# Regrouping the weight transform of a frequency-domain convolution: groups of four frequencies, three matmuls of 160 columns per PSUM bank

## The chip, the cores and the metric

The kernel runs on one core of a Trainium2 chip. The metric is the device time of one execution in microseconds (us). The time before is the median of three runs, 275.3 us, with a lowest of 274.16 us and a highest of 279.05 us. The profile is of one further execution, which took 277.49 us and whose span from the first to the last instruction was 275.8 us.

## The reference

```
H = W = 224; C = 96; K = 7            # x: (1, 224, 224, 96) bf16, w: (7, 7, 96, 96) bf16
wp = pad w with zeros to (224, 224, 96, 96)
Xf = rfft2(x over H and W); Wf = rfft2(wp over H and W)
Yf = einsum('bhwi,hwio->bhwo', Xf, Wf)
y  = irfft2(Yf) as bf16                # (1, 224, 224, 96)
```

This is a circular 7 x 7 convolution of an image of 96 channels into 96 channels. Every output channel sums over every input channel, tap by tap.

## The kernel before, in words

**What is computed where.** The rows are cut into 8 blocks (NJ) of 28 output rows. Each block is transformed along H by a short transform of length 34, which gives NS = 17 frequencies; frequency 0 carries two real parts, every other one three parts (real, imaginary, and a difference of the two, so that a complex product takes three real ones). Along W the kernel stays in the position domain and works with taps: the 7 taps and three sums of neighbouring taps, NTAP = 10, used on even positions, odd positions and their differences. The width is cut into 7 tiles of 32 pixels. For each tile t and frequency s, `b_round(t, s)` does the products over the 96 input channels: 33 matmuls of 96 columns (22 for frequency 0) with the pixels as the stationary operand and the transformed weights `WF` as the moving one. ScalarE scales the first bank (`tt_`), VectorE makes `u` and `v`, GpSimd (for some rounds VectorE) adds them into `yf`, and after each group of frequencies `yf` goes to a scratch tensor in DRAM, from which `tt` is read back in another layout for the inverse transform (`Gm`) and the output.

**Forward transform of the pixels.** Matmuls with `Fm` on pixel rows (`xn`) put the frequencies of a tile into PSUM, and an eviction writes them to `xf`. VectorE then makes the planes of differences and sums, `J`, for a group of three frequencies at a time (`jit`).

**Transform of the weights, where the change is.** `WF` holds, for each of 50 slots (frequency and part) and 10 taps, a 96 x 96 matrix. It is made once, group by group of frequencies (`PGRP`, line 31). `prep_jobs(gi)` (lines 322 to 359) makes one job per PSUM bank. A job takes hb pairs of output channels; for each pair one matmul has the raw weights `wq` as stationary operand, 98 rows by 128 columns, whose columns stand 96 elements (192 bytes) apart (`wqx[0:PW2, o:o + 127 * C + 1:C]`, line 340), and as moving operand the small table `Em`, which selects taps and multiplies by cosines and sines. Each matmul gives both channels of the pair, 10 taps, and two parts of each frequency of the group. One eviction per bank, from fp32 in PSUM to bf16, then writes hb neighbouring output channels for each slot and tap:

```
evac(wv[:, :, 0:2 * NTAP, :, o0:o1],
     pv_.rearrange("i k h (s q) -> i s q h k", s=ns), NB * ncol)
```

so the innermost run of the write is hb elements of bf16, starting at element o0 = ob * hb of a row of 48. The third part of each frequency is a subtraction on VectorE over 960 elements (`diff(s)`, line 353). In all groups before, NB = 8 and hb = 4: twelve banks to a group, four matmuls to a bank. A group of three frequencies has matmuls of 2 x 3 x 2 x 10 = 120 columns and evictions of 480 elements; group 0 (frequencies 0 and 1, all five slots) has matmuls of 100 columns.

**What sets the order.** Everything is recorded in program order; there is no other scheduler. Tiles 0 and 1 run together, tile 1 four rounds behind (LAG = 4): round r does frequency r of tile 0, and from r = 4 also frequency r - 4 of tile 1. A clock k counts two steps per round (k = 2r, 2r + 1). Every batch of jobs is entered with `add(a, b, jobs)` and `pace` hands it out evenly over steps a to b - 1, in the middle and at the end of a round (`mid`, `end`). Group gi of the weights is due in the rounds of the group before it:

```
add(2 * PGRP[gi - 1][0], 2 * PGRP[gi - 1][1] - 1, pj)
...
k = 2 * (PGRP[gi][0] + i) - 2          # the subtraction of a frequency: one round ahead of its use
```

Before, group 2 is made in rounds 2 to 4, groups 3, 4 and 5 in rounds 5 to 7, 8 to 10 and 11 to 13. `f_jobs` and the copies of a halo bring tile 1's pixels in during rounds 1 to 6, and tile 2's from round 9.

**Which engine evicts.** `evac` (line 122) keeps a running cost of VectorE and ScalarE (`load`) and gives each eviction to the one that is behind; `load["p"]`, the cost of TensorE's work, lifts both when they lag behind it. So an eviction may change engine when the costs before it change.

**When the raw weights' memory is given up.** At r = PGRP[-2][1] + 1 the pool that holds `wq` is closed and the tiles for the inverse transform take its place; two GpSimd memsets (`GA`, `GB`) follow.

Of the kernel before, what the change touches and what calls it, by code (L numbers as in the profile page):

```python
# [25 lines left out]
NB = 8  # L26
# [1 line left out]
NTAP = 10  # L28
TAPS = ((7, 8, 9, 6), (0, 2, 4, 6), (1, 3, 5))
NSLOT = 2 + 3 * (NS - 1)  # L30
PGRP = ((0, 2), (2, 5), (5, 8), (8, 11), (11, 14), (14, 17))
YGRP = ((0, 3), (3, 6), (6, 9), (9, 12), (12, 15), (15, 17))
YGRPL = ((0, 3), (3, 6), (6, 9), (9, 12), (12, 15), (15, 17))
SA = 9
# [13 lines left out]
def slot(s, part):  # L48
    return part if s == 0 else 2 + 3 * (s - 1) + part
# [3 lines left out]
def kernel(  # L53
# [54 lines left out]
    def bank():  # L108
        return pools["psb"].tile([128, 512], F32, name="pb")
# [5 lines left out]
    def apart(key, zone, r):  # L115
        for z, q in parts.setdefault(key, []):
            if z != zone and q.engine != r.ins.engine:
                tc.declare_no_dep(r.ins, q, reason="disjoint parts of one tile")
        parts[key].append((zone, r.ins))
        return r  # L120

    def evac(out_ap, in_ap, n):
        if tail[0]:
            return tail_evac(out_ap, in_ap, n)
        cv, ca = 180 + 1.0 * n, 160 + 0.85 * n
        for k in "va":
            load[k] = max(load[k], load["p"])
        if load["v"] + cv <= load["a"] + ca:
            load["v"] += cv
            return VE.tensor_copy(out=out_ap, in_=in_ap)  # L130
        load["a"] += ca
        return SE.copy(out=out_ap, in_=in_ap)
# [34 lines left out]
    xh_bufs = [late[:, 2 * (XW + 32) + i * XHW:2 * (XW + 32) + (i + 1) * XHW] for i in range(2)]  # L167
    assert 2 * (XW + 32 + XHW) <= 8 * NTAP * C and NSLOT - 8 > slot(PGRP[-1][0], 0)

# [109 lines left out]
    VE.tensor_tensor(out=pv[:, :, 2], in0=pv[:, :, 0], in1=pv[:, :, 1], op=ALU.subtract)  # L279
    for k0, k1 in ((0, slot(PGRP[0][1], 0)), (slot(PGRP[0][1], 0), NSLOT)):  # L280
        VE.tensor_tensor(out=Em[:, :, k0:k1], in0=pe3[:, k0:k1].unsqueeze(1).unsqueeze(3).to_broadcast([PW2, 2, k1 - k0, NTAP]),
# [40 lines left out]
    def prep_jobs(gi):  # L322
        s0, s1 = PGRP[gi]
        ns = s1 - s0
        full = gi == 0
        ncol = (NSLOT_OF(s0, s1) if full else 2 * ns) * NTAP
        nb = C // NB
        hb = NB // 2
        assert NB * ncol <= 512 and C2 % hb == 0

        def mk_(ob):
            def f():
                pw = bank()
                pv_ = pw[:, 0:NB * ncol].rearrange("p (k h q) -> p k h q", h=2, q=ncol)
                ev = Em[:, :, slot(s0, 0):slot(s1 - 1, 2) + 1, :]
                ev = ev.rearrange("p h a t -> p h (a t)") if full else ev.rearrange("p h (s r) t -> p h s (r t)", r=3)[:, :, :, 0:2 * NTAP]
                load["p"] += 63.0 * hb
                for k in range(hb):
                    o = ob * hb + k
                    TE.matmul(pv_[:, k], lhsT=wqx[0:PW2, o:o + 127 * C + 1:C], rhs=ev, start=True, stop=True)  # L340
                pv_ = pv_[0:C]
                o0, o1 = ob * hb, (ob + 1) * hb
                wv = WF[0:C, slot(s0, 0):slot(s1 - 1, 2) + 1]
                if full:
                    wv = wv.rearrange("i a t (h o) -> i (a t) h o", h=2)
                    apart(("W", gi), ob, evac(wv[..., o0:o1], pv_.rearrange("i k h q -> i q h k"), NB * ncol))
                    return
                wv = wv.rearrange("i (s r) t (h o) -> i s (r t) h o", r=3, h=2)
                apart(("W", gi), ob, evac(wv[:, :, 0:2 * NTAP, :, o0:o1],
                      pv_.rearrange("i k h (s q) -> i s q h k", s=ns), NB * ncol))  # L350
            return f

        def diff(s):
            def f():
                load["v"] += 250 + C * NTAP / 1.92
                w0, w1, w2 = (WF[0:C, slot(s, r)].rearrange("i t o -> i (t o)") for r in range(3))
                VE.tensor_tensor(out=w2, in0=w0, in1=w1, op=ALU.subtract)
            return f
        return [mk_(ob) for ob in range(nb)], [] if full else [diff(s) for s in range(s0, s1)]

    def NSLOT_OF(s0, s1):
        return slot(s1 - 1, 2) + 1 - slot(s0, 0)
# [3 lines left out]
    def new_xf(t, s0=0, s1=NS):  # L366
        xf = xf_bufs[t % 2]
        xf_tiles[t] = xf
        if t > 0:
            prev = xf_tiles[t - 1]  # L370
            for ph in range(2):
                o, i = (v[0:C, ph, :, s0:s1, p:p + HALO, :].rearrange("c r s w j -> c r s (w j)") for v, p in ((xf, 0), (prev, TW)))
                apart(("A", t), ("halo", s0), SE.copy(out=o, in_=i))
                load["a"] += 160 + 0.85 * 2 * (s1 - s0) * HALO * NJ
        return xf
# [35 lines left out]
    def then_load(f, t, jg):  # L411
        def g():
            f()
            if t < NT:
                load_x(t, jg)
        return g
# [262 lines left out]
    def queue_c(t):  # L679
        pend.extend((t, *k) for k in LT)  # L680
        pump()
# [11 lines left out]
    for f in prep_jobs(0)[0]:  # L693
        f()
# [22 lines left out]
    def fills(qs, k):  # L717
        def f():
            for q in qs:
                pace(q, k)  # L720
        return f

    qs = []

    def add(a, b, jobs):
        qs.append([a, b, jobs, len(jobs)])

    for gi in range(1, len(PGRP)):
        pj, dj = prep_jobs(gi)
        add(2 * PGRP[gi - 1][0], 2 * PGRP[gi - 1][1] - 1, pj)  # L730
        for i, f in enumerate(dj):
            k = 2 * (PGRP[gi][0] + i) - 2
            add(k, k + 1, [f])
# [11 lines left out]
    for r in range(NS + LAG):  # L745
        if r == 0:
            add(0, 4, fj[1][1])
        for p in range(2):
            if r == (1, 3)[p]:
                new_xf(1, SH2[1][p], SH2[1][p + 1])  # L750
                fj = f_jobs(1, p)
                if p == 1:
                    for jg in range(2):
                        fj[jg][-1] = then_load(fj[jg][-1], 2, jg)
                add(2 * r + 1, 2 * r + (5, 8)[p], fj[0] + fj[1])
        for p in range(3):
            if r == (9, 14, 17)[p]:
                new_xf(2, SH2[2][p], SH2[2][p + 1])
                fj = f_jobs(2, p)
                if p == 2:  # L760
                    for jg in range(2):
                        fj[jg][-1] = then_load(fj[jg][-1], 3, jg)
                add(2 * r, 2 * r + (8, 7, 5)[p], fj[0] + fj[1])
        if r == PGRP[-2][1] + 1:
            assert not any(q[2] for q in qs[:4 * len(PGRP) - 8])
            wtmp_cm.__exit__(None, None, None)
            t_pool = ctx.enter_context(tc.tile_pool(name="tt", bufs=NTT, side="right"))
            t2_pool = ctx.enter_context(tc.tile_pool(name="tt2", bufs=1, side="right"))
            yo_pool = ctx.enter_context(tc.tile_pool(name="yo", bufs=2, side="right"))
            g_pool = ctx.enter_context(tc.tile_pool(name="gp", bufs=1, side="right"))  # L770
            GA = g_pool.tile([KA, 4 * B], BF16, name="GA")
            GB = g_pool.tile([128, 2, 4 * B], BF16, name="GB")
            GE.memset(GA[:], 0.0)
            GE.memset(GB[:], 0.0)
        if r == NS + 3:
            queue_c(0)
        for t in range(2):
            s = r - LAG * t
            if not 0 <= s < NS:
                continue  # L780
            now = bursts.pop((r, t), ())
            now = jit(*now) if now else ()
            both = LAG <= r < NS
            b_round(t, s, fills(qs, 2 * r + (t if both else 0)), fills(qs, 2 * r + (t if both else 1)), False, now)
# [8 lines left out]
    for t in range(2, NT):  # L793
# [6 lines left out]
        qs = []  # L800
# [100 lines left out]
```

## Time and profile before

| engine | busy, us | share of the span | instructions |
|---|---|---|---|
| TensorE, matmuls | 260.8 | 95% | 5088 |
| TensorE, weight loads | 238.9 | 87% | 5088 |
| VectorE | 227.8 | 83% | 469 |
| ScalarE | 196.3 | 71% | 475 |
| GpSimd | 102.2 | 37% | 152 |

The busy time of an engine is the union of its instructions' times, and matmuls overlap each other: one is listed at some 200 ns, while the next starts 42 ns later. So the distance from one start to the next, not the listed duration, tells what a matmul costs in a stream. The shares are means over stages with different limits. The chip's profile has 288 matmuls on `wq` (48 of 100 columns, 240 of 120 columns), between 18.4 and 80.2 us of the span. The rounds of tiles 0 and 1 fill the span from about 24 to 103 us; tiles 2 to 6 follow, 17 rounds each.

### The profile page before, as it was taken

How to read it: one execution, taken by the hardware profiler on the slowest of the kernel's cores; microseconds unless marked ns; L12 is line 12 of the kernel's file. 1: busy time of each engine (PE TensorE's matmuls, PEld its weight loads, DVE VectorE, ACT ScalarE, POOL GpSimd, SP SyncE). 2: the span in 40 equal slices, each digit the busy share in tenths (PEclk: the TensorE clock that was granted, in tenths of full speed). 3: DMA queues.
4: the chain of work that ended last, by engine and by line, in shares of the span. 5: the costliest groups of instructions: out<-in, count | busy, mean ns of one | idle time of the engine just before them, and what ended most of it. 6: DMA issues, size and time to landing. Idle time of an engine off the chain costs nothing.

```text
span 275.8 us, 12056 instructions
## 1 busy us (share of the span) xinstructions
PE 260.8 (95%) x5088; PEld 238.9 (87%) x5088; DVE 227.8 (83%) x469; ACT 196.3 (71%) x475; POOL 102.2 (37%) x152
## 2 busy tenths in 40 slices
PE   8969999989998999999999999999999999999972
PEld 3649998989998999899999999999999999999751
DVE  5528999998999889977976897788988889899933
ACT  5518997768774566898988869888887874653522
POOL 7720033445446455233243215222432242654200
PEclk9988999999999999999999999999999999999999
DMA  6954313411111189787979487977949833979775
GB/s 176 239 99 128 88 48 108 146 50 48 45 60 67 55 243 191 198 244 230 315 211 256 131 239 222 220 200 200 295 132 180 275 124 110 206 213 241 185 185 181
DMA packets 46211, 46.79 MB, mean 170 GB/s; under 512 B 35274, under 2 KB 37846, under 8 KB 46058
## 3 DMA queue, kind: packets, MB, share of 16 engines
q1 hardware_dynamic: 45692, 44.34, 59.3%
q0 software_dynamic: 464, 1.67, 1.8%
q8 instruction: 40, 0.66, 1.1%
q14 instruction: 15, 0.12, 0.1%
HBM read 24.65 MB, written 21.33 MB: 167 GB/s over the span
## 4 chain that ended last, share of the span: by engine, by line
PE 56%; DVE 17%; DMA 12%; issue 6%; ACT 4%; POOL 3%; SPq 2%; DVEq 0%
PE pb L87 56%; DVE J L87 6%; DMA wq<-in_w_dram 5%; DMA tt<-scr 5%; DVE WF L87 4%; DVE v L87 3%; POOL yf L87 3%; DVE u L87 2%; SPq L87 2%; ACT xf L87 2%; DMA xf<-scrl 2%; ACT WF L87 1%; DVE yf L87 1%; DVE yo L87 0%; DVE xf L87 0%
## 5 line engine op out<-in xcount | busy, mean ns | idle before, releaser
L87 PE MATMUL pb<-WF,J 96*128 96x96 bf16 x2898 | 167.6, 206 | 1.4 <-DVE J L87 0.6
L87 PEld LDWEIGHTS <-J 96*128 96x128 bf16 x2898 | 141.5, 98 | 10.7 <-DVE J L87 1.7
L87 POOL TENSOR_TENSOR yf<-v,u 128x384 bf16<-128x384 f32 x85 | 85.2, 1018 | 141.7 <-issue 84.8
L87 ACT CAST xf<-pb 96x408 bf16<-96x408 f32 (+5 forms) x142 | 66.9, 492 | 7.8 <-PE pb L87 5.8
L87 PE MATMUL pb<-WF,xf 96*128 96x96 bf16 x952 | 61.0, 206 | 2.9 <-DVE WF L87 2.1
L87 DVE TENSOR_TENSOR J<-xf 96x1824 bf16<-96x1824 bf16 (+1 forms) x84 | 60.3, 756 | 0.1
L87 PEld LDWEIGHTS <-xf 96*128 96x128 bf16 x952 | 47.4, 98 | 3.8 <-issue 3.1
L87 PE MATMUL pb<-Fm,xn 118*128 118x136 bf16 (+4 forms) x576 | 44.5, 203 | 0.0
L87 ACT CAST WF<-pb 96x480 bf16<-96x480 f32 (+1 forms) x60 | 30.0, 561 | 8.4 <-PE pb L87 8.1
L87 PE MATMUL pb<-tt,Gm 102*84 102x384 bf16 (+1 forms) x132 | 33.6, 327 | 0.0
L87 PEld LDWEIGHTS <-xn 118*128 118x128 bf16 x576 | 29.2, 98 | 0.1
L87 ACT CAST yo<-pb 84x384 bf16<-84x384 f32 (+1 forms) x61 | 26.3, 480 | 4.1 <-PE pb L87 4.0
L87 ACT CAST J<-pb 84x384 bf16<-84x384 f32 (+1 forms) x62 | 26.8, 482 | 2.7 <-PE pb L87 2.7
L87 DVE TENSOR_TENSOR J<-J 96x912 bf16<-96x912 bf16 (+1 forms) x42 | 24.9, 594 | 0.0
L87 PE MATMUL pb<-wq 98*128 98x120 bf16 (+1 forms) x288 | 22.9, 234 | 2.1 <-DMA wq<-in_w_dram 2.1
L87 PEld LDWEIGHTS <-wq 98*128 98x128 bf16 x288 | 20.5, 151 | 2.5 <-issue 2.5
L87 PE MATMUL pb<-wu 128*128 128x512 bf16 (+3 forms) x70 | 18.7, 398 | 1.1 <-DVE ct L87 1.1
L87 DVE TENSOR_TENSOR yf<-v,u 128x384 bf16<-128x384 f32 x27 | 15.6, 578 | 0.9
L87 DVE TENSOR_TENSOR WF<-WF 96x960 bf16<-96x960 bf16 x15 | 15.8, 1057 | 0.2
L87 PEld LDWEIGHTS <-wu 128*128 128x128 bf16 (+3 forms) x70 | 7.9, 115 | 8.4 <-issue 2.9
L87 DVE CAST WF<-pb 96x400 bf16<-96x400 f32 (+1 forms) x12 | 7.2, 608 | 8.4 <-PE pb L87 8.1
L87 PEld LDWEIGHTS <-Gm 102*84 102x84 bf16 (+1 forms) x132 | 11.5, 117 | 1.7 <-issue 0.6
(394 smaller groups left out, 236.9 us busy)
## 6 DMA issues: line engine op xcount, KB each, us to landing
scr<-yf SPq DMA_DIRECT2D x30, 288.0 KB
xn<-in_x_dram SPq DMA_DIRECT2D x12, 672.0 KB
tt<-scr SPq DMA_DIRECT2D x24, 336.0 KB
out_dram<-yo SPq DMA_DIRECT2D x12, 252.0 KB
out_dram<-J SPq DMA_DIRECT2D x12, 252.0 KB
tt<-scr SPq DMA_DIRECT2D x6, 288.0 KB
wq<-in_w_dram SPq DMA_DIRECT2D x1, 1719.0 KB
scrl<-yf POOLq DMA_DIRECT2D x5, 288.0 KB, 5.1
```

Source lines behind the costliest of these rows:

```text
L87: r = fn(*a, **k)
```

## The change

From group 2 on, a weight group has four frequencies instead of three. A matmul then has 2 x 4 x 2 x 10 = 160 columns, and since a PSUM bank holds 512 fp32 values, three of them fit instead of four: NB is 6 instead of 8 for these groups, hb is 3 instead of 4, and there are 16 banks to a group. The eviction of a bank still has 480 elements. There are five groups instead of six. The purpose is to make the same transformed weights with fewer matmuls and weight loads. An assertion is put in terms of the due step instead of an index.

```diff
-PGRP = ((0, 2), (2, 5), (5, 8), (8, 11), (11, 14), (14, 17))
+PGRP = ((0, 2), (2, 5), (5, 9), (9, 13), (13, 17))
@@ prep_jobs
         ncol = (NSLOT_OF(s0, s1) if full else 2 * ns) * NTAP
+        NB = 8 if ns < 4 else 6
         nb = C // NB
         hb = NB // 2
@@ rounds of tiles 0 and 1
         if r == PGRP[-2][1] + 1:
-            assert not any(q[2] for q in qs[:4 * len(PGRP) - 8])
+            assert not any(q[2] for q in qs if q[1] <= 2 * r)
```

## The prediction

> **What bounds the kernel now.** I read the page's slices first, to see which engine is full where the weights are made (18 to 80 us, slices 3 to 12).
>
> ```profile
> PE   8969999989998999999999999999999999999972
> DVE  5528999998999889977976897788988889899933
> ACT  5518997768774566898988869888887874653522
> ```
>
> Each digit is a fortieth of the span, 6.9 us. From slice 14 on TensorE is full and VectorE is not: TensorE sets the pace of tiles 2 to 6, which the change does not touch. From 28 to 62 us VectorE is as full as TensorE. So I asked for the busy time in stretches that end with the `v` of one round or two of tiles 0 and 1:
>
> ```profile
> 32.54:36.30 3.76, 3.76 (x91) 3.76 (x90) 3.76 (x8) 3.76 (x9) 1.57 (x1) 1.00 0.01 2
> 36.30:39.87 3.57, 3.57 (x83) 3.50 (x82) 3.15 (x7) 3.57 (x10) 1.00 (x1) 1.00 0.23 87
> 39.87:44.26 4.39, 3.85 (x87) 3.60 (x86) 4.29 (x9) 3.09 (x10) 1.39 (x2) 1.00 0.34 85
> 44.26:49.16 4.90, 4.90 (x112) 4.90 (x111) 4.90 (x9) 4.21 (x11) 1.66 (x2) 1.00 0.25 80
> 49.16:54.26 5.10, 5.10 (x119) 5.10 (x118) 5.02 (x10) 4.37 (x11) 1.65 (x2) 1.00 0.45 133
> ...
> 62.31:67.22 4.91, 4.91 (x118) 4.91 (x117) 4.50 (x8) 4.43 (x11) 1.93 (x3) 1.00 0.17 63
> ```
>
> After the stretch and its length stand the busy us of TensorE, its weight loads, VectorE, ScalarE and GpSimd. The first three rows are rounds 2, 3 and 4: VectorE idles 0 + 0.42 + 0.10 us of 11.7, ScalarE 0 + 0 + 1.30. Rounds 5 and 6 (next two rows): VectorE idles 0.08 of 10.0, ScalarE 1.42. In rounds 9 to 12 (62.31 to 80.25 us, one row shown) VectorE idles 1.27 of 17.9. **VectorE bounds rounds 2 to 8, ScalarE beside it in rounds 2 and 3; in rounds 9 to 12 VectorE and TensorE are both near full.** The idle time before TensorE's work agrees: in this stage it waits for the weights' subtraction on VectorE, not the other way round.
>
> ```profile
> 43.38 0.33 PE L87 MATMUL pb<-WF,xf 96*128 96x96 bf16 x4 [0.24 <-DVE WF L87]
> 61.17 0.33 PE L87 MATMUL pb<-WF,xf 96*128 96x96 bf16 x4 [0.79 <-DVE WF L87]
> ```
>
> (timeline: start, length, what, and in brackets the idle time and who ended it).
>
> Now the pieces that change, from the timeline and from the groups by shape between 28 and 90 us:
>
> ```profile
> 47.06 0.93 PE L87 MATMUL pb<-WF,J 96*128 96x96 bf16 x18
> 28.28 1.16 PE L87 MATMUL pb<-wq 98*128 98x120 bf16 x16
> 18.45 0.83 PE L87 MATMUL pb<-wq 98*128 98x100 bf16 x10 [2.08 <-DMA wq<-in_w_dram]
> ```
>
> ```profile
> L87 PEld LDWEIGHTS <-J 96*128 96x128 bf16 x665 | 31.2, 98 | 0.6 <-DVE WF L87 0.4
> L87 ACT CAST WF<-pb 96x480 bf16<-96x480 f32 x49 | 24.8, 570 | 0.0
> L87 DVE TENSOR_TENSOR WF<-WF 96x960 bf16<-96x960 bf16 x15 | 15.8, 1057 | 0.2
> L87 PEld LDWEIGHTS <-wq 98*128 98x128 bf16 x208 | 14.6, 149 | 0.0
> L87 DVE CAST WF<-pb 96x480 bf16<-96x480 f32 x5 | 3.1, 644 | 0.0
> ```
>
> A merged row of n matmuls ends one duration after the last start, so the spacing is (length - duration) / (n - 1). Products of 96 columns: (0.93 - 0.206) / 17 = 43 ns. `wq` with 120 columns, 227 ns each: (1.16 - 0.227) / 15 = 62 ns. `wq` with 100 columns, some 0.22 us each: (0.83 - 0.22) / 9 = 68 ns. Fewer columns are no faster, so the weight load, not the columns, sets this spacing; the 98 ns loads behind 43 ns products against 149 ns loads here say the same.
>
> **What the Trainium skill says.** "TensorE: Matmul & The Clock Gate", section "LDWEIGHTS (loading the stationary operand)": a load's time goes by its columns alone. The trace disagrees: both loads above have 128 columns, and one takes 98 ns, the other 149. "SBUF — State Buffer", section "Specifications (TRN2)", has the likely reason: full rate needs at least two accesses per 16-byte line, and the columns of `wq` are 192 bytes apart. "Vector Engine (DVE) Microarchitecture Reference", section "5.2 Measured stream behaviour on trn2 (trn3 not measured)", says that a port keeps its rate only in runs of two adjacent 4-byte words that start on an 8-byte boundary: 1.054 ns per column then, 1.30 when both sources start on an odd word, 2.50 when each element of dst hops by 24 words. Runs of four bf16 are exactly 8 aligned bytes, and the trace agrees that they are free: on ScalarE 480 elements take 570 ns and a plain 384 takes 483, so 0.9 ns an element. Runs of three are 6 bytes, and no row of before has them. Lastly "SBUF — State Buffer", section "Who interferes with whom": a VectorE instruction with two SBUF inputs contends with GpSimd's reads. The subtraction takes 637 to 1458 ns in this trace, so a shift in time alone can move a round by some tenths.
>
> **The change part by part.**
> *TensorE.* Groups 2 to 5 had 4 x 12 banks x 4 = 192 matmuls of 120 columns; now 3 x 16 x 3 = 144 of 160. The cost of a column: products of 384 columns at the end start 165 ns apart, so (165 - 43) / 288 = 0.42 ns, and 160 columns cost 43 + 64 x 0.42 = 70 ns if the load (62 ns) hides behind them. Saved: 192 x 62 - 144 x 70 = 1.8 us. If instead the load's excess over the columns (62 - 53 = 9 ns) stays on top, 79 ns and 0.5 us. I take 1.8.
> *Where it lies.* Laid out by the code's steps, the banks of rounds 2 to 13 go from 5 5 2, 5 5 2, 5 5 2, 5 5 2 to 7 6 3, 5 5 4, 2 5 5, 4 2 0. Rounds 2 to 4 get four banks more, and TensorE 48 matmuls of 70 ns for 48 of 62: 0.4 us more. Rounds 5 and 6 save 40 x 62 - 30 x 70 = 0.4 us, rounds 9 to 12 save 68 x 62 - 48 x 70 = 0.9.
> *Evictions.* 48 of 480 elements before and after. By the running costs of `evac`, VectorE takes two of the four extra ones (rounds 3 and 4) and ScalarE two. VectorE starts its next work 0.57 us after one (timeline, 38.16 to 38.73), so it gets 1.14 us more in a stretch where it idles 0.52, and 0.42 of that is a wait for ScalarE, itself full there. The subtraction for frequency 5 is queued behind them on VectorE, and TensorE waits for it (the row at 43.38). I take **+0.9** (0.6 to 1.14).
> *Given back.* In round 6 one `xf` eviction of 516 ns goes from VectorE to ScalarE, which idles 1.42 us there: **-0.5** (0 to -0.5). In rounds 7 and 8 VectorE's work is the same: 0, since ScalarE's extra eviction meets 1.87 us of its idle time. In rounds 9 to 12 TensorE's 0.9 us counts only where VectorE does not follow at once; VectorE's idle spans there end on GpSimd's `yf`, not on TensorE: **-0.2** (0 to -0.9). Rounds 13 and 14: ScalarE loses two evictions and TensorE eight matmuls, while VectorE is full in 83.31 to 87.76: 0.
> *Runs of three.* They start at byte 6 x ob, so half of the banks (ob mod 4 = 1 or 2) have every run across an 8-byte boundary. Priced as an odd start, 1.30 / 1.054 = 1.23 times: 0.11 us more on VectorE's 500 ns of elements, 0.09 on ScalarE's 400 (an estimate from that page, ScalarE by analogy). In rounds 2 to 4 that is two such of VectorE's four and six of ScalarE's twelve: 0.2 and 0.5 us on engines already full, **+0.3**; later they lie in ScalarE's idle time. Bounds: free, and the rival below.
> *No cost:* the fifteen subtractions keep their steps; GpSimd's two memsets (0.19 and 0.28 us) come a round earlier, into idle time; four evictions in tiles 4 and 5 go from VectorE to ScalarE, where TensorE is full.
> Sum: 0.9 - 0.5 - 0.2 + 0.3 = +0.5, so 275.3 + 0.5 = **275.8 us**.
>
> **The rivals.**
> *TensorE is the real bound and VectorE only looks full.* For it: TensorE is full in five of the six rows above. Against it: its waits end on VectorE. It then gains what TensorE saves: 275.3 - 1.8 = 273.5.
> *The early rounds lose all and nothing comes back:* +1.14 for VectorE and +0.5 for the runs, 277.0. For it: nothing idles in rounds 2 and 3. Against: round 6 loses an eviction.
> *Runs of three are dear, so the kernel is slower.* For it: the one write here with a hop after every bf16, `Fm`, takes 762 ns for 136 elements, where another two-source operation on 170 takes 336. That is some 3.4 ns an element on top, though GpSimd may hold it up for part of it. At 4.4 ns for each 8 bytes touched a run costs 4.4 or 8.8 ns instead of 3.1, on average 2.1 times; at 2.5 ns, 1.3 times. At 1.7 times ScalarE pays 0.28 us an eviction: 12 x 0.28 = 3.4 us in rounds 2 to 4, and 32 x 0.28 = 9 in rounds 5 to 12, against 7.1 us of its idle time there, 2 more: 275.8 + 5.4 = 281.2. At 2.1 times, 287. Against it: three accesses fall on most lines.
>
> **How the numbers follow.** Forecast 0.50, TensorE as the bound 0.20, early loss 0.18, dear runs 0.12. The range, 273.2 to 278.5, takes in the first three and the scatter of a median of three, and leaves out most of the last and a little below. More than 2% faster (under 269.8) is beyond what TensorE can save: 0.02. More than 2% slower (over 280.8) needs the dear runs: 0.09. Within 2%: 0.89.
>
> **What would show it.** `wq` spacing near 70 ns; WF evictions at 570 to 660 ns on ScalarE; the `v` of round 4 later by about 1 us, half of it back by round 6, and tile 2's start within 1 us of before. WF evictions above 800 ns would prove the dear runs; a round 12 that ends 1.5 us early would prove the forecast wrong in favour of TensorE.

## The result and the profile after

The changed kernel takes 286.76 us (median of four, 285.17 to 287.36), the kernel before 276.9 us (median of four in the same comparison). The ratio is **1.040**, with a 95% interval of 1.031 to 1.049: slower by about 10 us, above the range that was forecast (273.2 to 278.5 us, built on the 275.3 us that the kernel before had in three runs). It ends near the rival "runs of three are dear".

The page's slices of the changed kernel, to be held against those of before:

```profile
PE   8879888998986899999999999999999999999973
DVE  5539968868749988977988788877988889989934
ACT  6439998999994365788798878988798885553423
```

ScalarE now reads 9 or 8 from slice 4 to 12, where VectorE did; VectorE and TensorE have holes there. The busy times in rounds 2, 3, 4, 5, 6 and 9, cut at the same work as the six rows of before (after the stretch and its length: TensorE, weight loads, VectorE, ScalarE, GpSimd, in us):

```profile
31.05:34.82 3.77, 3.02 (x63) 2.83 (x61) 3.77 (x8) 3.77 (x6) 1.55 (x1) 1.00 0.01 2
34.82:41.32 6.50, 5.22 (x101) 4.63 (x99) 4.06 (x8) 6.50 (x12) 0.99 (x1) 1.00 0.13 49
41.32:48.09 6.77, 5.31 (x100) 4.67 (x97) 5.63 (x11) 5.36 (x13) 1.38 (x2) 1.00 0.23 64
48.09:53.01 4.92, 4.71 (x101) 4.61 (x100) 4.92 (x10) 4.92 (x9) 1.66 (x2) 1.00 0.22 62
53.01:57.96 4.95, 4.89 (x99) 4.63 (x98) 3.98 (x8) 4.95 (x11) 1.65 (x2) 1.00 0.36 93
...
67.30:72.21 4.91, 4.62 (x105) 4.53 (x104) 4.50 (x8) 4.91 (x8) 1.93 (x3) 1.00 0.18 63
```

ScalarE is busy all the time in five of the six. Round 3 takes 6.50 us instead of 3.57, round 4 takes 6.77 instead of 4.39. The groups by shape from 30 us on, where all evictions of the weights are in runs of three, name the reason: they still have 480 elements.

```profile
L87 ACT CAST WF<-pb 96x480 bf16<-96x480 f32 x44 | 40.3, 1065 | 0.0
L87 DVE CAST WF<-pb 96x480 bf16<-96x480 f32 x4 | 3.7, 975 | 0.0
```

One takes 1065 ns on ScalarE where it took 570, and 975 on VectorE where it took 644. (The expectations below say 1043 ns: that mean is over a stretch that begins at 28 us and takes in two evictions of group 1, still in runs of four.) ScalarE's busy time per eviction, from the busy time and the count, goes from 24.8 / 49 = 0.51 us to 40.3 / 44 = 0.92: **0.41 us more each**. How that reaches the path is seen in the timelines, first of ScalarE, then of VectorE, in round 3:

```profile
34.93 1.94 ACT L87 CAST WF<-pb 96x480 bf16<-96x480 f32 x2
36.63 0.67 ACT L87 CAST xf<-pb 96x512 bf16<-96x512 f32 x1
37.18 1.01 ACT L87 COPY xf<-xf 96x432 bf16<-96x432 bf16 x2
38.08 0.42 ACT L87 ACTIVATE tt__825<-pb 128x288 f32<-128x288 f32 x1
```

```profile
38.60 0.36 DVE L87 SCALAR_TENSOR_TENSOR u<-pb,tt__825 128x192 f32<-128x192 f32 x1 [2.44 <-ACT tt__825 L87]
38.88 0.64 DVE L87 TENSOR_TENSOR WF<-WF 96x960 bf16<-96x960 bf16 x1
```

ScalarE takes its work in the order in which the kernel records it. The round's `tt_` (`tt__825`) stands there behind the evictions and two copies of the halo, and `u` on VectorE waits 2.44 us for it, and with `u` all that VectorE has to do after. TensorE in turn finds its PSUM banks or its weights not ready (13 waits on a ScalarE `WF` eviction, 5.1 us in all between 28 and 95 us, none before). By stages, cut where VectorE ends the last `v` of a round (in round 4 and in the last row the `yf` of a frequency 0):

| rounds | before, us | after, us | difference |
|---|---|---|---|
| 2 to 4 | 11.72 | 17.04 | +5.32 |
| 5 and 6 | 10.00 | 9.87 | -0.13 |
| 7 and 8 | 8.05 | 9.34 | +1.29 |
| 9 to 12 | 17.94 | 21.72 | +3.78 |
| 13 to 20, and round 0 of tile 2 | 22.89 | 22.89 | 0 |

The sum, 10.3 us, agrees with the loss of the medians, 9.9 us. The two profiled runs themselves differ by 7.6 us in span, because outside the table the changed kernel's run was 2.7 us shorter: 1.5 us ahead of round 2, where both do the same work but the granted clock was 0.74 between 20 and 25 us before and 1.00 after, and 1.2 us behind these rounds. In rounds 9 to 12 ScalarE is now the limit: its busy time rises from 15.26 to 19.59 us, though it makes 16 evictions there instead of 17, and it does not idle at all until the last bank is out. Of the 2.7 us that it had to spare before (17.94 - 15.26), 2.1 still stand idle, but behind the last bank, where they help nothing.

### The profile page after: what moved, and what is told of

The parts are those of the page before. It is cut to its first block, busy times and chain, and to the rows that moved or that the text cites. A ratio compares the mean times of both kernels' runs of the same rounds, so it can differ in the third digit from the quotient of the medians.

```text
span 283.4 us, 11958 instructions
## 1 busy us (share of the span) xinstructions
PE 261.8 (92%) x5040; PEld 237.9 (84%) x5040; DVE 224.3 (79%) x466; ACT 211.6 (75%) x478; POOL 102.3 (36%) x152
## 4 chain that ended last, share of the span: by engine, by line
PE 44%; DVE 12%; issue 4%; DMA 4%; POOL 2%; ACT 1%; SPq 1%; DVEq 0%; ACTq 0%; POOLq 0%
PE pb L87 44%; DVE J L87 6%; DVE v L87 3%; DMA xf<-scrl 3%; POOL yf L87 2%; DVE yf L87 2%; DVE u L87 1%; DMA scrl<-yf 1%; SPq L87 1%; ACT WF L87 1%; DVE yo L87 0%; DVE WF L87 0%; DVE tt L87 0%; DVEq L897 0%; ACT tt__2844 L87 0%
## 5 line engine op out<-in xcount | busy, mean ns | idle before, releaser
L87 ACT CAST xf<-pb 96x408 bf16<-96x408 f32 (+5 forms) x145 | 68.9, 494 | 6.4 <-PE pb L87 4.6
L87 DVE TENSOR_TENSOR J<-xf 96x1824 bf16<-96x1824 bf16 (+1 forms) x84 | 59.4, 746 | 0.1
L87 ACT CAST WF<-pb 96x480 bf16<-96x480 f32 (+1 forms) x58 | 47.0, 936 | 7.7 <-PE pb L87 7.6
L87 PE MATMUL pb<-Fm,xn 118*128 118x136 bf16 (+4 forms) x576 | 45.1, 203 | 1.9 <-ACT WF L87 1.6
L87 PEld LDWEIGHTS <-xn 118*128 118x128 bf16 x576 | 29.8, 97 | 2.9 <-issue 2.8
L87 PE MATMUL pb<-wq 98*128 98x160 bf16 (+2 forms) x240 | 21.5, 233 | 3.6 <-DMA wq<-in_w_dram 2.0
L87 PEld LDWEIGHTS <-wq 98*128 98x128 bf16 x240 | 18.3, 146 | 4.5 <-DMA wq<-in_w_dram 2.4
L87 PE MATMUL pb<-wu 128*128 128x512 bf16 (+3 forms) x70 | 17.9, 382 | 1.1 <-DVE ct L87 1.1
L87 DVE CAST WF<-pb 96x480 bf16<-96x480 f32 (+1 forms) x14 | 9.3, 706 | 7.7 <-PE pb L87 7.7
L87 DVE TENSOR_TENSOR WF<-WF 96x960 bf16<-96x960 bf16 x15 | 12.7, 844 | 1.9 <-ACT WF L87 1.7
```

Of the source, the lines that this page charges most:

```text
L87: r = fn(*a, **k)
```

## The experiments

The theory after the result: a write in runs of three bf16 is what makes the evictions dear. Rivals: the wider steps of the PSUM read (640 and 320 bytes instead of 480 and 240), and the order (four more banks in rounds 2 to 4).

**Long runs, same groups.** The pair of output channels that one matmul makes is 2o and 2o + 1 instead of o and o + 48. The two rows of `Em` then interleave, and a bank writes one run of six where it wrote two runs of three:

```diff
-[[C * C, n], [C2, 2], [1, WC]]                    # wq: second half of the rows 48 channels on
+[[C * C, n], [1, 2], [1, WC]]                     # one channel on
-lhsT=wqx[0:PW2, o:o + 127 * C + 1:C]
+lhsT=wqx[0:PW2, 2 * o:2 * o + 127 * C + 1:C]
-evac(wv[:, :, 0:2 * NTAP, :, o0:o1], pv_.rearrange("i k h (s q) -> i s q h k", s=ns), NB * ncol)
+evac(wv[:, :, 0:2 * NTAP, o0:o1, :], pv_.rearrange("i k h (s q) -> i s q k h", s=ns), NB * ncol)
```

(Cut to the lines that matter, with comments added; `wv` is split to match, group 0 is changed in the same way, and `Em` moves 48 columns on, to stand behind the longer rows of `wq`.)

> The changed kernel, but the pair of output channels of one matmul is 2o and 2o+1 instead of o and o+48, so that a bank's eviction writes one run of six bf16 where it wrote two runs of three. Matmuls, banks, their order and the 640 and 320 byte steps of the PSUM read stay. Theory of the runs (the write of three bf16 at a time is what is dear): evictions of 480 elements fall from 1043 ns on ScalarE to under 650 ns, and the time falls from 286.8 us to 275 to 277. Theory of the reads (the wider steps in PSUM are what is dear): evictions stay above 900 ns and the time at 285 or more. Theory of the order (four more banks in rounds 2 to 4 are what is dear): evictions may change, but rounds 2 to 4 stay 4 us longer than before.

Measured: **276.29 us**, before 276.61 in the same comparison, ratio 1.0007 (0.9979 to 1.0035). The groups by shape over the whole run, and the busy times in rounds 2 to 4, 5 and 6, 7 and 8, 9 to 12:

```profile
L87 ACT CAST WF<-pb 96x480 bf16<-96x480 f32 x52 | 26.3, 577 | 0.1
L87 DVE CAST WF<-pb 96x480 bf16<-96x480 f32 x8 | 5.0, 642 | 0.0
```

```profile
30.10:43.27 13.17, 12.15 (x253) 11.60 (x252) 13.06 (x25) 11.42 (x28) 3.39 (x4) 1.00 0.18 52
43.27:52.85 9.58, 9.58 (x209) 9.55 (x208) 9.56 (x17) 8.64 (x21) 3.31 (x4) 1.00 0.36 98
52.85:60.92 8.07, 6.88 (x146) 6.78 (x143) 7.68 (x14) 4.90 (x13) 4.00 (x5) 1.00 0.30 98
60.92:78.86 17.94, 17.94 (x412) 17.94 (x410) 16.48 (x30) 14.40 (x32) 7.91 (x9) 1.00 0.14 52
```

The evictions are cheap again and the whole loss is gone, with the same matmuls, the same PSUM steps and the same banks in the same rounds. The reads and the order are out as its cause. What the grouping is worth by itself stands in these rows too: +1.45 us in rounds 2 to 4 (13.17 - 11.72), -0.42 in rounds 5 and 6, +0.02 and 0.00 after. In all it is worth nothing that the interval can tell. Of the 1.45 us, 0.84 lie in round 2 (4.60 us, before 3.76), and they have nothing to do with evictions. They come from one subtraction of the weights on VectorE:

```profile
32.12 1.00 POOL L87 TENSOR_TENSOR yf<-v,u 128x384 bf16<-128x384 f32 x1 [9.94 <-DVE J L87]
32.16 1.48 DVE L87 TENSOR_TENSOR WF<-WF 96x960 bf16<-96x960 bf16 x1
```

It starts 0.04 us after GpSimd's sum and takes 1.48 us. In the profile of before the same two start at 34.56 and 34.60 us, and there the subtraction takes 0.64 us and GpSimd's sum 1.57. So one profile can put such a stage off by most of a microsecond: with groups of three, rounds 2 to 4 took 11.72 us in the profile of before, and 12.30 and 11.79 in those of two kernels below (long runs in the kernel before; shift by two).

**Runs of three alone.** Groups of three as before, and `NB = 8 if full else 6`.

> The kernel before with its groups of three frequencies, and only NB = 6 behind group 0: three matmuls of 120 columns per bank, 80 late banks instead of 60, evictions of 360 elements in runs of three, PSUM steps of 480 and 240 bytes as before. Theory of the runs: about 1043 x 360 / 480 = 780 ns on ScalarE for one eviction, where a cheap one of 360 elements takes 549. Theory of the reads: about 470 to 550 ns. The time is well above before in the first case (80 x 780 ns is some 62 us of evictions against 34), 277 to 280 us in the second.

Measured: 285.39 us in a single run; the kernel before has 276.61. The groups by shape between 28 and 95 us:

```profile
L87 ACT CAST WF<-pb 96x360 bf16<-96x360 f32 x64 | 44.0, 852 | 0.0
L87 ACT CAST xf<-pb 96x360 bf16<-96x360 f32 x8 | 3.8, 537 | 0.0
```

The same engine, the same 360 elements, both from PSUM: 852 ns in runs of three, 537 in runs of four. The PSUM steps are those of before. The `xf` evictions read PSUM in another order, but the reads of the `WF` evictions are those of before, where they were cheap. So the write is dear on its own.

**Long runs in the kernel before.** The same edit of the channel pairs with groups of three: runs of eight.

> The kernel before with the pair of channels 2o and 2o+1: one run of eight bf16 where two runs of four were written. Theory of the runs: runs of four were already free, so the evictions stay at 540 to 580 ns and the time within 1 us of before. Beside the run on the changed kernel it shows what the grouping is worth when no run is short.

Measured: 276.38 us, ratio 0.9987 (0.9961 to 1.0013); ScalarE's evictions took 568 ns. So runs of four were no dearer than runs of eight.

**The place of a run.** The kernel before with `WF` one bf16 further on in its tile, so that each run of four covers one whole 4-byte word and half of the word on each side of it:

```diff
+WFb = cpool.tile([128, NSLOT * NTAP * C + 8], BF16, name="WF")
+WF = WFb[:, 1:1 + NSLOT * NTAP * C].rearrange("p (a t o) -> p a t o", a=NSLOT, t=NTAP)
```

(Cut; the pixel buffers that borrow the end of the tile keep their place.)

> The kernel before with the whole tile WF one bf16 element further on: runs of four as before, but each starts 2 bytes past a multiple of 8 and crosses an 8-byte boundary (3 + 1 elements), every second one a 16-byte line. If the place of a run is what costs, evictions of 480 elements rise from 570 ns to 800 or more on ScalarE, those that cross a 16-byte line more than the others; if only the length of three is dear, they stay below 620 ns. The matmuls and the subtraction that read WF may change as well, so the time is not compared.

Measured: evictions of 480 elements took 1065 ns on ScalarE on average and 1080 on VectorE; the single run took 293.95 us. Two that follow each other on ScalarE's timeline:

```profile
52.40 0.72 ACT L87 CAST WF<-pb 96x480 bf16<-96x480 f32 x1
...
52.97 1.27 ACT L87 CAST WF<-pb 96x480 bf16<-96x480 f32 x1
```

The first is of a bank whose runs lie within a 16-byte line, the second of one whose runs cross a line, and so it alternates through the group. So a length of three is not needed: on average four elements are as dear as three when they start on an odd one. The average hides a difference, though. Within a line these evictions took 712 to 946 ns on ScalarE, with two words written in part to a run; runs of three within a line, in the changed kernel, took 905 to 1127, with one. The price is not a fixed sum for each such word.

**The place by whole words.** The same with a shift of two elements: whole 4-byte words, but across an 8-byte boundary, and in every second bank across a 16-byte line.

> The kernel before with the whole tile WF two bf16 elements (4 bytes) further on: runs of four that start 4 bytes past a multiple of 8, on whole 4-byte words, every second one across a 16-byte line. Theory of the words (what is dear is a 4-byte word that a run writes only in part): evictions stay at 540 to 600 ns on ScalarE and the time within 2 us of before. Theory of the lines (what is dear is to cross an 8-byte boundary or a 16-byte line): evictions rise as with a shift by one element, to 700 ns and to 1250 ns where a line is crossed, and the time is above 285 us.

Measured: 276.41 us in a single run; the kernel before has 277.38 in the same comparison.

```profile
L87 ACT CAST WF<-pb 96x480 bf16<-96x480 f32 x54 | 28.4, 590 | 0.1
L87 DVE CAST WF<-pb 96x480 bf16<-96x480 f32 x6 | 3.8, 646 | 0.0
```

590 ns against 570, and VectorE as before. Crossing an 8-byte boundary costs nothing here, and crossing a line little: what was dear is the **4-byte word that a run writes only in part**. Three bf16 always leave one such word; four leave two when they start on an odd element. How the price counts (by word, by run or by line) no run here settles.

**Short runs of whole words.** The changed kernel with `NB = 4` for groups of four: runs of two.

> The changed kernel with two matmuls of 160 columns per bank instead of three: groups of four frequencies, 24 banks to a group, 96 late evictions of which 72 have 320 elements, in runs of two bf16, one whole 4-byte word that never crosses an 8-byte boundary. Theory of the words: about 320 x 0.84 + 165 = 435 ns for one on ScalarE. Theory of the short runs (a run costs some 4 ns or more however short it is): 160 runs x 4.1 ns + 165 = 820 ns. The time is above before in both, since there are 24 more evictions: 276 to 281 us in the first case, above 285 in the second.

Measured: 279.41 us in a single run; the kernel before has 277.38. The groups by shape between 28 and 95 us:

```profile
L87 ACT CAST WF<-pb 96x320 bf16<-96x320 f32 x64 | 28.8, 585 | 0.0
L87 ACT CAST xf<-pb 96x320 bf16<-96x320 f32 x6 | 2.4, 416 | 0.0
```

It falls between the two theories: 585 ns against the 435 of the words and the 820 of the short runs. Some of that is the listing, since the duration grows along an unbroken series: in one such series 531, 544, 557, 571 ns, while the starts stay 0.38 us apart. The first of a series, 527 to 545 ns, is still 0.1 us above the 416 of `xf`. So a run of one whole word costs a little, 0.1 us / 160 runs = 0.7 ns each, and two bf16 are cheaper to evict per run than three.

**Fewer banks in rounds 2 to 4.** Long runs, and the groups cut so that rounds 2 to 4 have 8 banks instead of 12 (shown against the kernel before, without the edit of the channel pairs):

```diff
-PGRP = ((0, 2), (2, 5), (5, 8), (8, 11), (11, 14), (14, 17))
+PGRP = ((0, 2), (2, 5), (5, 7), (7, 10), (10, 13), (13, 17))
+NB = 8 if full else {2: 12, 3: 8, 4: 6}[ns]
```

> The kernel before with channel pairs 2o and 2o+1 (no short runs) and the groups 0-1, 2-4, 5-6, 7-9, 10-12, 13-16, so that rounds 2 to 4 make 8 banks instead of 12 (the changed kernel: 16), and later rounds make four more. Evictions in all as before. Theory that VectorE and ScalarE bound rounds 2 to 4 and idle later: rounds 2 to 4 get 1.0 to 1.5 us shorter, rounds 5 and 6 up to 0.5 us longer, the time 275.4 to 276.2 us where the same with groups of three has 276.4. Theory that the place of the evictions costs nothing: the same time within 0.3 us and rounds 2 to 4 as before.

Measured: 279.12 us, before 277.38 in the same comparison, ratio 1.0062 (1.0034 to 1.0090), so 0.6% slower; the expectation failed. Rounds 2 to 4, then 5 and 6, in its profile:

```profile
31.93:44.26 12.33, 11.14 (x260) 11.04 (x259) 11.11 (x22) 9.85 (x24) 4.33 (x4) 1.00 0.26 79
44.26:54.81 10.55, 10.45 (x231) 10.35 (x230) 9.70 (x20) 8.64 (x22) 2.88 (x4) 1.00 0.28 79
```

Rounds 2 to 4 are not shorter (12.33, before 11.72), and rounds 5 and 6 are 0.55 longer. A bank of this group has six matmuls instead of four, so TensorE has the same 48 weight matmuls in rounds 2 to 4 as before, and 48 instead of 40 in rounds 5 and 6. That evictions alone bound rounds 2 to 4 is refuted: taking four away gained nothing in the sum. The trace shows what took their place. Round 2 is shorter, 3.17 us instead of 3.76. In round 3 (4.34 us instead of 3.57) `u` on VectorE waits 1.22 us for `tt_` on ScalarE, 0.42 before: there it stands behind two evictions of `xf` and two copies of the halo, which are left as they were. In round 4 (4.82 us instead of 4.39) the subtraction starts 0.10 us after GpSimd's sum and takes 1.40 us instead of 0.66.

## Why the prediction was wrong

- **What bounds the kernel:** for rounds 7 to 12 the run with long runs shows that it is not TensorE's weight matmuls: there are fewer, and the rounds take 8.07 and 17.94 us, before 8.05 and 17.94. For rounds 2 to 4 "VectorE, ScalarE beside it" names the right engines, but the last experiment shows that the number of evictions does not set their length: ScalarE's other work and the subtraction's meeting with GpSimd do as much.
- **TensorE's saving:** a `wq` row of nine 160-column matmuls takes 0.85 us, at 239 ns each, so (0.85 - 0.239) / 8 = 76 ns, not 70. The saving is 192 x 62 - 144 x 76 = 1.0 us, not 1.8. It brings nothing, where the forecast counted 0.2.
- **The early banks:** forecast +0.9 us, measured +1.45 with long runs, but not by the mechanism alone: 0.84 of it is the subtraction in round 2. The two evictions more on VectorE, in rounds 3 and 4, stand beside +0.05 and +0.56 us, so about 0.6, the lower end of the range. **Given back in rounds 5 and 6:** -0.5, measured -0.42. **Rounds 9 to 12:** -0.2, measured 0.00. **Rounds 13 on:** 0, measured 0.
- **The step that failed is "Runs of three".** It priced them like an odd start, 1.23 times, on half of the banks, so 0.09 us on ScalarE and 0.11 on VectorE, +0.3 us in rounds 2 to 4 and the rest hidden. The runs showed 0.41 us on ScalarE, as the mean over all banks, and the term is worth 9.2 us instead of 0.3: rounds 2 to 12 take 57.97 us in the changed kernel and 48.76 with long runs. The overlap failed with the price: the evictions filled ScalarE's idle time, which the forecast counted as room, and then went on the path through `tt_`.
- **The rival on it** had the right effect and nearly the right size (0.44 us and 287 us at 2.1 times; its own sum, 12 x 0.44 + 32 x 0.44 - 7.1 on top of 275.8, gives 288), but got 0.12 of the chances. That 287 is so near 286.76 is in part luck. The hint was in the profile of before: `Fm`, written one bf16 at a time, at 762 ns. Its mechanism, so many ns for each 8 bytes touched, was wrong: the shift by two elements touches two such pieces per run and is nearly free.
- **The Trainium skill's rule** in section 5.2 of "Vector Engine (DVE) Microarchitecture Reference", full rate only in runs that start on an 8-byte boundary, was not seen in these writes: runs of four bf16 that start 4 bytes past one took 646 ns on VectorE, before 644. Its table is of 4-byte elements and could not show partial words. And its row for an odd start, from which the 1.23 times came, is of two sources, not of a destination.
- The effect named beforehand as proof, `WF` evictions above 800 ns, is what came.

## What to carry to other kernels

When a change alters how many elements an engine writes side by side, price the write, not the element count. In evictions like these, keep every run of bf16 on whole 4-byte words (an even start and an even length). If a blocking factor becomes odd, first see whether a different assignment of rows or channels makes the runs twice as long; here that one edit took away the whole loss. And idle time of an engine that takes its work in order is no free room, if something that others wait for stands behind the work put there.

## What the runs showed of the hardware that was not expected

- A bf16 write from PSUM to SBUF with partial 4-byte words is slow on both engines: on ScalarE 480 elements took 570 ns in aligned runs of four, 1065 in runs of three, 1065 in runs of four from an odd element; on VectorE 644, 975 and 1080.
- With partial words, crossing a 16-byte line costs more still. In the run with the shift by one, evictions took 712 to 946 ns on ScalarE within a line and 1261 to 1421 across one. In the last group of the changed kernel, all on ScalarE, the banks numbered 2, 5, 10 and 13, whose runs start 12 or 14 bytes into a line, took 1197 to 1346 ns, and the other twelve 906 to 1090. With whole words a line crossed cost ScalarE some 0.04 us for 480 elements (the run with the shift by two).
- A weight load of 128 columns 192 bytes apart takes 149 ns, one of 128 neighbouring columns 98, and with it matmuls start about 62 ns apart whether they have 120 columns or, in the last experiment, 80; at 160 columns the spacing is 76, still 6 ns above what the columns alone were priced at.
